# The second batch's sums of r*u*k made on TensorE per pair of heads, in a fused linear attention and gated feed-forward kernel

## The chip, the cores and the metric

The kernel runs on one core of one Trainium2 chip, as one launch. The metric is the device time of that launch in microseconds (us), the median of several runs. The engines are named as in the profile: PE is TensorE, DVE is VectorE, ACT is ScalarE, POOL is GpSimd, and SP issues the DMAs.

## The reference

Three layers follow each other on 4 batches of 768 tokens with 384 features. The change lies in the first, a linear attention with 8 heads of 48 features and a decaying state:

```python
for t in range(S):
    cur = einsum('bhd,bhe->bhde', u[None] * k_t, v_t)
    y[:, :, t] = einsum('bhd,bhde->bhe', r_t, state + cur)
    state = w_t[..., None] * state + einsum('bhd,bhe->bhde', k_t, v_t)
```

The token's own part, r_t times cur, is v_t times one number per token and head: the sum over the 48 features of r*u*k. These sums are what the change moves. Behind the attention come a feed-forward layer (h = gelu(x @ w_in), a layer norm of its second half, a 768x768 product over tokens, a gate, w_out, and a residual) and a second one (a sigmoid of a causal convolution with 5 taps, times x @ w_val, times w_out). All of it is fp32 to the reader; the large products are made as three products of split operands.

## The kernel before, in words

**Units and batches.** The attention is cut into units: one unit is one batch b, one segment s of 256 tokens (three per batch) and one pair p of heads (four), so 12 units per batch and 48 in all. Tokens of a segment lie in two tiles j of 128. Batch 0's attention runs first, with the loading and decoding of the weights and the start of its own feed-forward part beside it. After that `phase(b)` (L659) runs the feed-forward part of batch b, in the order of the words of `ORDER0`, `ORDER` or `LAST` (L646 to L657), and at each word `T` advances the attention of batch b + 1 by one tick. Batch 1's attention therefore runs beside batch 0's feed-forward part, which also still decodes weights (L144) and splits them into two parts (L161).

**The order of work.** The framework records the instructions, and a planner with a timing model orders each engine's queue by priorities and by when operands are ready in its model. `LEAD` (L112) moves the priority of each kind of step. On the chip each queue then runs in that order, and an instruction at its head that waits holds those behind it.

**One unit.** `unit` (L247) gives its steps. The packed tile `pk` holds decay, k and r with features on partitions. DVE makes the suffix products F (L271) and the prefix products E (L276), POOL makes r*E into L (L280), DVE (POOL for batch 0) makes k*F, called kh (L283). PE transposes kh (L297) and makes the scores (L303); ACT copies them, DVE masks (L311). In the next tick `kv` (L323) makes the chunk sums k*v on PE into one PSUM bank (L328), ACT copies them out (L347), a DVE scan runs the states (L353), ACT spreads them (L358), and another tick later PE makes the tokens' outputs (L372), which DVE adds to the tile `y` (L377). Batches 1 to 3 have two buffers for `pk`, and one for each of the two PSUM banks of `kv` and of the tokens.

**The token's own part** is made in two ways.
- Batch 0 (`first`): the step `q` makes r*k on DVE (L291), 128x256, in place over the decay part of `pk`. In `kv`, for each of the two tiles, PE multiplies it by a two-column matrix that holds u of the pair's two heads (L333), into columns of the same PSUM bank. The step `o` copies the four numbers per token out on ACT (L338), and POOL multiplies v by them into `y` (L342), 128x192 per unit.
- Batches 1 to 3: `bonus` (L222), once per tile of 128 tokens, six per batch, works on a tile `rk` with r and k of all heads, tokens on partitions. It is loaded by DMA (L220), into a single buffer. POOL makes r*k (L228), DVE multiplies by u (L229) and reduces over the features (L232), then the next load is issued, and POOL multiplies v by the sums into `y` (L236), 128x384 per tile. `begin` (L423) calls it for both tiles of a segment at its first pair.

**Queues and buffers nearby.** All DMAs are issued by SP, in its order: `pk`, `sv`, `v`, `rk`, weights and the output. `run_loads` (L396) issues the next load of a kind when its buffer's user is done. `y` and `v` have two buffers, one per segment. `y` is later transposed by PE for the feed-forward part (L470).

Of the kernel before, what the change touches and what calls it, by code (L numbers as in the profile page):

```python
# [26 lines left out]
SEG = 256  # L27
# [7 lines left out]
KS = S // 128  # L35
# [17 lines left out]
def tile_kernel(ctx, tc, pk, sv_, rk_, v_, u_, misc_, w_in, w_sgT, b_sg, w_o1, w_val,  # L53
# [39 lines left out]
    parts, at = {}, dict.fromkeys(ROOMS, 0)  # L93
# [9 lines left out]
    def buf(name, n, b=None):  # L103
        l = parts[name][min(units[n][0] if b is None else b, 1)]
        return l[n % len(l)]
# [20 lines left out]
    def leading(kind, f):  # L126
        def g(*args):
            with lead(kind):
                return f(*args)
        return g  # L130
# [44 lines left out]
    def load_weights(srcs, places):  # L175
        got = []
        for pl in dict.fromkeys(places):
            got += stage([s for s, p in zip(srcs, places) if p is pl], *pl)
        return got
# [33 lines left out]
    def load_nat(b, s):  # L213
        t = r2.tile([128, NT, DM], F32, tag="v", name="v")
        sp.dma_start(out=t, in_=v_[b, s * SEG:(s + 1) * SEG, :].rearrange("(j p) f -> p j f", p=128))
        vt[b, s] = t
# [5 lines left out]
    def bonus(b, i):  # L222

        s, j = divmod(i, NT)
        with lead("bon"):
            t = buf("rk", b * KS + i, b)
            q = t[:, 0:DM]
            pool.tensor_tensor(out=q, in0=q, in1=t[:, DM:2 * DM], op=ALU.mult)  # L228
            dve.tensor_tensor(out=q, in0=q, in1=u_bc, op=ALU.mult)  # L229
            hd = lambda a: a.rearrange("p (h d) -> p h d", d=D)  # L230
            rs = r2.tile([128, H], F32, tag="rsw", name="rs")
            dve.tensor_reduce(out=rs, in_=hd(q), op=ALU.add, axis=AX.X)  # L232
            run_loads("rk", b * KS + i + 1)
            if j == 0:
                yt[b, s] = ry.tile([128, NT, DM], F32, tag="y", name="y")
            pool.tensor_tensor(out=hd(yt[b, s][:, j, :]), in0=hd(vt[b, s][:, j, :]),  # L236
                               in1=rs.unsqueeze(2).to_broadcast([128, H, D]), op=ALU.mult)
# [9 lines left out]
    def unit(n):  # L247

        b, s, p = units[n]
        pkt = buf("pk", n)  # L250
        w, k, r = pkt[:, 0:OK_], pkt[:, OK_:OR_], pkt[:, OR_:OS_]
        kh, kn = buf("kh", n), buf("kn", n)
        sv = buf("sv", n).rearrange("p (c g e) -> p c g e", g=2, e=D)

        first = b == 0
        S = buf("SE", n).rearrange("p (c g e) -> p c g e", g=2, e=D)
        vcd = buf("vcd", n).rearrange("p (j c f) -> p j c f", j=NT, c=2)
        F, E, d1e = buf("F", n), buf("E", n), buf("D1E", n)  # L260
# [3 lines left out]
        half = [slice(0, 64), slice(64, 128)]  # L264
        e3 = E.rearrange("p (c t) -> p c t", t=W1)
        f3 = F[:, 1:NW + 1].rearrange("p (c t) -> p c t", t=W1)
        q = pkt[:, 0:SEG]
        t = {}

        def suffix():  # L270
# [48 lines left out]
        def warm(o, k):  # L319
            for _ in range(k if first else 0):  # L320
                pe.matmul(out=o[:, 256:512], lhsT=wsrc[:, 0:128], rhs=wsrc[:, 0:256], start=True, stop=True)

        def kv():  # L323
            t["b"] = ps(1, n, [128, 512])
            warm(t["b"], WB)
            for j in range(NT):
                for hh in range(2):
                    pe.matmul(out=t["b"][half[hh], 2 * j * D:(2 * j + 2) * D],  # L328
                              lhsT=kn[:, j * 128 + 64 * hh:j * 128 + 64 * hh + 64],
                              rhs=vcd[:, j, :, hh * D:(hh + 1) * D], start=True, stop=True)  # L330
            if first:
                for j in range(NT):
                    pe.matmul(out=t["b"][:, NC * D + 2 * j:NC * D + 2 * j + 2],  # L333
                              lhsT=q[:, j * 128:(j + 1) * 128], rhs=u_col[:, 2 * p:2 * p + 2], start=True, stop=True)
# [40 lines left out]
        def y_out():  # L375
# [3 lines left out]
        steps = {"F": suffix, "E": prefix, "L": r_part, "K": k_part, "D": chunk_decay, "q": ruk,  # L379
                "t": turn, "s": scores, "k": k_rows, "m": causal, "v": v_rows,  # L380
                "B": kv, "o": own_v, "d": kv_out, "a": states, "S": s_part, "p": keep,
                "C": tokens, "y": y_out}
        return {c: leading(c, f) for c, f in steps.items()}

    STAGES = "FELKD", "tskmv", "BdaSp", "Cy"

    def ps(i, n, shape):

        if units[n][0] == 0 and n % 2:
            return psC.tile(shape, F32, tag=f"c{i}", name=f"a{i}")  # L390
        return psA.tile(shape, F32, tag=f"a{i}", name=f"a{i}")

    loads = {"pk": load_unit, "sv": load_sv, "rk": load_rk}
    loaded, user = {"pk": 0, "sv": 0, "rk": KS}, {}

    def run_loads(kind, done, most=NU):  # L396

        while loaded[kind] < (B * KS if kind == "rk" else NU) and most > 0:
            n = loaded[kind]
            t = buf(kind, n, n // KS if kind == "rk" else None)  # L400
            if user.get(id(t), -1) >= done:
                break
            user[id(t)] = n
            loads[kind](n)
            loaded[kind] += 1
            most -= 1

    def attention(b):


        n0, n1 = b * NSEG * NP, (b + 1) * NSEG * NP
        if b == 0:
            first_loads()
        todo = {}

        def step(n, which):
            if n0 <= n < n1:
                if n not in todo:
                    todo[n] = unit(n)
                for c in which:  # L420
                    todo[n].pop(c)()

        def begin(n):  # L423
            if n < n1:
                _, s, p = units[n]
                step(n, STAGES[0])
                run_loads("pk", n + 1)
                if p == 0:
                    for j in range(NT):
                        bonus(b, s * NT + j)  # L430

        if b == 0:
            TICK = "F1 K1 E1 C-2 L1 q1 y-2 B-1 v1 d-1 o-1 t0 k0 s0 a-1 D1 S-1 p-1 m0"
            step(0, "FKEDLqv")
            for n in range(n0, n1 + 2):
                for w in TICK.split():
                    step(n + int(w[1:]), w[0])
                run_loads("sv", n - 1)
                run_loads("pk", min(n, n1))
                if 0 < n < n1 and units[n][2] == 0:  # L440
                    load_nat(*units[n + NP][0:2])
                yield
            return
        begin(n0)
        if n0 + NP < NU:
            load_nat(*units[n0 + NP][0:2])
        for n in range(n0, n1 + 2):
            for i in (2, 1, 0):
                step(n - i, STAGES[i + 1])
            run_loads("sv", n - 1)  # L450
            begin(n + 1)
            m = n + 1
            if m < min(n1, NU - NP) and units[m][2] == 0:
                load_nat(*units[m + NP][0:2])
            yield
# [203 lines left out]
    def phase(b):  # L659
        nx = b + 1 < B  # L660
        gen = attention(b + 1) if nx else None
        wgen = rest_of_weights() if b == 0 else iter(())
        own = {"u": u_step, "s": vs_step, "w": wo_step, "v": val_step, "o": out_step}
        for word in (ORDER0 if b == 0 else LAST if b == B - 1 else ORDER).split():
            kind, at = word[0], [int(x) for x in word[1:]]
            if kind in own:
                own[kind](b, *at)
                for _ in range(2):
                    next(wgen, None)
            elif kind == "i":  # L670
                x2_init(b, *at)
            elif kind == "c":
                for f in range(KD):
                    conv(b, at[0], f)
            elif nx:
                if kind == "T":
                    next(gen)
                elif kind == "n":
                    u_step(b + 1, 0, *at)
                else:  # L680
                    {"x": xT, "h": hv}[kind](b + 1, *at)
# [14 lines left out]
    def first_loads():  # L696
        ld = {"k": "pk", "s": "sv"}
        small = {"I": (ident, ident_), "M": (misc, misc_), "U": (u_bc, u_.to_broadcast([128, DM])),
                 "B": (b_bc, b_sg.to_broadcast([128, S]))}
        for c in "kMkvI s sk ks W kskvsk sks BU":  # L700
            if c in ld:
                run_loads(ld[c], 0, 1)
            elif c == "v":
                load_nat(0, len(vt))
            elif c in small:
                sp.dma_start(out=small[c][0], in_=small[c][1])
            elif c == "W":
                early["v"] = load_weights(cols(w_in, DV), [VN] * 3)
        for k in loads:
            run_loads(k, 0)  # L710

    att = attention(0)
    for n in range(14):
        next(att)
# [113 lines left out]
```

## Time and profile before

| what | value |
|---|---|
| runs of the kernel before (3) | median 584.35 us, 582.72 to 585.93 |
| the profiled execution, its own time | 586.35 us |
| its span, first to last instruction | 584.5 us |
| mean granted TensorE clock | 0.944 |
| PE busy | 524.6 us (90%), 4012 instructions |
| PE weight loads (PEld) busy | 446.8 us (76%), 4012 |
| DVE busy | 440.1 us (75%), 823 |
| ACT busy | 296.0 us (51%), 683 |
| POOL busy | 278.3 us (48%), 282 |
| moved by DMA | 55.76 MB, mean 95 GB/s |

The profile is of one execution, with every instruction's start and end on its engine. A busy PE is not PE at its peak, since matmuls are pipelined and their ends modelled. An instruction's time on DVE or POOL contains what it waits for inside it. Idle time ahead of an instruction is put down to whatever ended last before it. Line numbers are those of the kernel before; the names of tiles are given as output<-inputs.

### The profile page before, as it was taken

How to read it: one execution, taken by the hardware profiler on the slowest of the kernel's cores; microseconds unless marked ns; L12 is line 12 of the kernel's file. 1: busy time of each engine (PE TensorE's matmuls, PEld its weight loads, DVE VectorE, ACT ScalarE, POOL GpSimd, SP SyncE). 2: the span in 40 equal slices, each digit the busy share in tenths (PEclk: the TensorE clock that was granted, in tenths of full speed). 3: DMA queues.
4: the chain of work that ended last, by engine and by line, in shares of the span. 5: the costliest groups of instructions: out<-in, count | busy, mean ns of one | idle time of the engine just before them, and what ended most of it. 6: DMA issues, size and time to landing. Idle time of an engine off the chain costs nothing.

```text
span 584.5 us, 10613 instructions
## 1 busy us (share of the span) xinstructions
PE 524.6 (90%) x4012; PEld 446.8 (76%) x4012; DVE 440.1 (75%) x823; ACT 296.0 (51%) x683; POOL 278.3 (48%) x282
## 2 busy tenths in 40 slices
PE   8787888889747999889998998999999998999996
PEld 4565665788636898679877887889877887999985
DVE  7999999988997648993399659984399359523774
ACT  4766947542745435653365555654266635422233
POOL 7578845684666126662154126672154124722630
PEclk9899787978869999999997999899999999999999
DMA  8952444433434231342105351242104100000002
GB/s 313 385 218 56 150 151 121 151 109 108 123 91 139 85 107 42 96 127 77 42 9 156 96 156 34 60 159 82 42 15 116 61 16 0 28 14 1 1 0 81
DMA packets 27937, 55.76 MB, mean 95 GB/s; under 512 B 3184, under 2 KB 17264, under 8 KB 27888
## 3 DMA queue, kind: packets, MB, share of 16 engines
q1 hardware_dynamic: 27888, 55.11, 29.6%
q8 instruction: 31, 0.51, 0.4%
q14 instruction: 18, 0.15, 0.1%
HBM read 50.38 MB, written 4.72 MB: 94 GB/s over the span
## 4 chain that ended last, share of the span: by engine, by line
PE 48%; DVE 16%; issue 2%; ACT 1%; DMA 1%; POOL 1%; POOLq 0%; ACTq 0%
PE vps L514 13%; DVE cv L607 8%; PE ups L514 6%; PE c L578 6%; PE o L633 6%; PE val L514 4%; PE hv L491 4%; PE a L372 4%; PE a L303 2%; PE a L328 2%; DVE x L589 1%; PE a L297 1%; DVE SD L353 1%; DVE bs L497 1%; DVE vg L503 1%
## 5 line engine op out<-in xcount | busy, mean ns | idle before, releaser
L514 PE MATMUL vps<-wsg,vnt 128*128 128x384 f32 x576 | 116.7, 346 | 5.1 <-POOL wsg L164 3.2
L514 PEld LDWEIGHTS vps<-wsg,vnt 128*128 128x128 f32 x576 | 102.5, 193 | 8.3 <-POOL wsg L164 3.7
L565 POOL TENSOR_TENSOR gt<-gt,ut 128x384 f32<-128x384 f32 x32 | 35.0, 1096 | 110.5 <-DVE gt L554 90.2
L607 DVE SCALAR_TENSOR_TENSOR cv<-x,cw_col,cv 128x384 f32<-128x384 f32 x96 | 76.9, 835 | 0.0
L491 PE MATMUL hv<-win,x 128*128 128x512 f32 x216 | 64.9, 435 | 4.8 <-DVE cv L620 2.9
L578 PE MATMUL c<-gl,late 128*128 128x384 f32 x288 | 63.0, 348 | 1.6 <-DVE gl L568 1.3
L514 PE MATMUL ups<-x,win 128*128 128x384 f32 x288 | 61.4, 355 | 0.0
L358 ACT ACTIVATE SE<-SD 64x192 f32<-64x192 f32 x80 | 44.8, 560 | 28.1 <-DVE SD L353 13.2
L280 POOL TENSOR_TENSOR L<-pk,E 128x256 f32<-128x256 f32 x38 | 30.4, 800 | 51.1 <-PE a L372 32.9
L514 PEld LDWEIGHTS ups<-x,win 128*128 128x128 f32 x288 | 52.6, 196 | 1.8 <-DVE spare L151 0.2
L578 PEld LDWEIGHTS c<-gl,late 128*128 128x128 f32 x288 | 50.3, 191 | 3.9 <-DVE gl L568 1.4
L491 PEld LDWEIGHTS hv<-win,x 128*128 128x128 f32 x216 | 41.8, 204 | 14.1 <-DVE cv L620 3.3
L353 DVE TENSOR_TENSOR_SCAN SD<-SD,SD 128x288 f32<-128x288 f32 x48 | 46.1, 962 | 7.3 <-ACT SD L347 7.1
L514 PE MATMUL val<-x2hl,late 128*128 128x384 f32 x216 | 45.6, 354 | 3.0 <-DVE gt L554 2.8
L633 PE MATMUL o<-late,ml 128*128 128x384 f32 x216 | 44.0, 342 | 2.1 <-DVE ml L623 2.1
L316 ACT ACTIVATE vcd<-v 64x192 f32<-64x192 f32 x84 | 30.0, 357 | 28.8 <-PE a L328 28.2
L271 DVE TENSOR_TENSOR_SCAN F<-pk,D1F 128x260 f32<-128x260 f32 x40 | 36.4, 911 | 9.9 <-DMA pk<-in_pk_dram 6.9
L514 PEld LDWEIGHTS val<-x2hl,late 128*128 128x128 f32 x216 | 38.6, 195 | 6.2 <-issue 3.1
L372 PE MATMUL a<-SE,L 128*64 128x96 f32 x304 | 31.9, 276 | 12.1 <-DVE x L474 6.8
L567 ACT ACTIVATE gl<-gt 128x384 fp32r<-128x384 f32 x32 | 16.7, 523 | 50.7 <-POOL gt L565 47.0
L554 DVE SCALAR_TENSOR_TENSOR gt<-vps,misc,b_bc 128x384 f32<-128x384 f32 x32 | 19.5, 610 | 28.6 <-PE vps L514 27.0
L507 POOL TENSOR_TENSOR vnt<-vg,vnt 128x512 fp32r<-128x512 f32 x24 | 33.8, 1412 | 15.1 <-ACT vnt L506 15.0
(148 smaller groups left out, 1088.8 us busy)
## 6 DMA issues: line engine op xcount, KB each, us to landing
pk<-in_pk_dram SPq DMA_DIRECT2D x40, 386.5 KB, 3.4
sv<-in_sv_dram SPq DMA_DIRECT2D x39, 192.0 KB, 2.5
rk<-in_rk_dram SPq DMA_DIRECT2D x18, 384.0 KB, 3.2
v<-in_v_dram SPq DMA_DIRECT2D x12, 384.0 KB, 3.5
out_dram<-ot SPq DMA_DIRECT2D x24, 192.0 KB, 1.9
bits<-in_w_in_dram SPq DMA_DIRECT2D x6, 512.0 KB, 6.7
room_l<-in_pk_dram SPq DMA_DIRECT2D x7, 386.5 KB, 6.3
bits<-in_w_o_dram SPq DMA_DIRECT2D x7, 384.0 KB, 4.6
```

Source lines behind the costliest of these rows:

```text
L271: dve.tensor_tensor_scan(out=F[:, NW:0:-1], data0=w[:, NW:0:-1], data1=D1F[:, NW:0:-1], initial=0.0, op0=ALU.mult, op1=ALU.add)
L280: pool.tensor_tensor(out=ch(L[:, 0, :]), in0=ch(r), in1=e3[:, :, 0:C], op=ALU.mult)
L353: dve.tensor_tensor_scan(out=SD1, data0=SD1, data1=SD0, initial=0.0, op0=ALU.add, op1=ALU.mult)
L358: act.activation(out=S[half[hh], :, hh, :], func=AF.Copy, in_=d1[half[hh], :, 1:NC + 1].rearrange("p e c -> p c e"))
L372: pe.matmul(out=o, lhsT=L[:, i, c * C:(c + 1) * C], rhs=rhs[:, c], start=(i == 0), stop=(i == 1))
L491: pe.matmul(out=ps, lhsT=x[:, a, kk, j * 128:(j + 1) * 128], rhs=win[:, w, kk, DV:2 * DV], start=(z == 0), stop=(z == nmm - 1))
L507: pool.tensor_tensor(out=vnt[b][:, 1, i, :], in0=vg, in1=hi.bitcast(F32), op=ALU.subtract)]
L514: pe.matmul(out=ps, lhsT=lhs(a, kk), rhs=rhs(w, kk), start=(z == 0), stop=(z == nk * 3 - 1))
L565: pool.tensor_tensor(out=t, in0=t, in1=ut.pop((b, hf, d)), op=ALU.mult)
L578: pe.matmul(out=acc[0][f], lhsT=late["wo1"][:, a, d, f * 128:(f + 1) * 128], rhs=g[:, w, :], start=(d == 0 and q == 0), stop=(d == KV - 1 ...
L607: dve.scalar_tensor_tensor(out=t, in0=x2[:, f, k:k + HALF], scalar=cw_col[:, f, k:k + 1], in1=t, op0=ALU.mult, op1=ALU.add)
L633: pe.matmul(out=acc2[0][j], lhsT=m[:, a, j * 128:(j + 1) * 128], rhs=late["wo2"][:, w, g, :], start=(g == 0 and q == 0), stop=(g == KD - 1 ...
```

## The change

Batch 1 takes batch 0's way: its units get the steps `q` and `o`, and `bonus` runs for batches 2 and 3 only. The product r*k, which for batch 0 overwrites the decay in `pk`, goes for batch 1 into thirds of the single buffer of `rk`, unit n into third n modulo 3. The first load of `rk` is that of batch 2's first tile, and it is issued when batch 2's attention begins and no longer ahead of everything in `first_loads`. In batch 1 the step `q` comes right after the unit's other preparing steps, and `o` after the states of the same unit.

```diff
--- before.py
+++ after.py
@@ -254,7 +254,7 @@
-        first = b == 0
+        first, summed = b == 0, b < SUMMED
         S = buf("SE", n).rearrange("p (c g e) -> p c g e", g=2, e=D)
         vcd = buf("vcd", n).rearrange("p (j c f) -> p j c f", j=NT, c=2)
         F, E, d1e = buf("F", n), buf("E", n), buf("D1E", n)
@@ -264,7 +264,7 @@
         half = [slice(0, 64), slice(64, 128)]
         e3 = E.rearrange("p (c t) -> p c t", t=W1)
         f3 = F[:, 1:NW + 1].rearrange("p (c t) -> p c t", t=W1)
-        q = pkt[:, 0:SEG]
+        q = pkt[:, 0:SEG] if first else parts["rk"][1][0][:, n % 3 * SEG:(n % 3 + 1) * SEG]
         t = {}
         def suffix():
@@ -328,7 +328,7 @@
                     pe.matmul(out=t["b"][half[hh], 2 * j * D:(2 * j + 2) * D],
                               lhsT=kn[:, j * 128 + 64 * hh:j * 128 + 64 * hh + 64],
                               rhs=vcd[:, j, :, hh * D:(hh + 1) * D], start=True, stop=True)
-            if first:
+            if summed:
                 for j in range(NT):
                     pe.matmul(out=t["b"][:, NC * D + 2 * j:NC * D + 2 * j + 2],
                               lhsT=q[:, j * 128:(j + 1) * 128], rhs=u_col[:, 2 * p:2 * p + 2], start=True, stop=True)
@@ -382,6 +382,8 @@
                 "C": tokens, "y": y_out}
         return {c: leading(c, f) for c, f in steps.items()}
+
+    SUMMED = 2
     STAGES = "FELKD", "tskmv", "BdaSp", "Cy"
     def ps(i, n, shape):
@@ -391,7 +393,7 @@
         return psA.tile(shape, F32, tag=f"a{i}", name=f"a{i}")
     loads = {"pk": load_unit, "sv": load_sv, "rk": load_rk}
-    loaded, user = {"pk": 0, "sv": 0, "rk": KS}, {}
+    loaded, user = {"pk": 0, "sv": 0, "rk": SUMMED * KS}, {}
     def run_loads(kind, done, most=NU):
@@ -424,8 +426,10 @@
             if n < n1:
                 _, s, p = units[n]
                 step(n, STAGES[0])
+                if b < SUMMED:
+                    step(n, "q")
                 run_loads("pk", n + 1)
-                if p == 0:
+                if p == 0 and b >= SUMMED:
                     for j in range(NT):
                         bonus(b, s * NT + j)
@@ -441,12 +445,16 @@
                     load_nat(*units[n + NP][0:2])
                 yield
             return
+        if b == SUMMED:
+            run_loads("rk", 0)
         begin(n0)
         if n0 + NP < NU:
             load_nat(*units[n0 + NP][0:2])
         for n in range(n0, n1 + 2):
             for i in (2, 1, 0):
                 step(n - i, STAGES[i + 1])
+                if i == 1 and b < SUMMED:
+                    step(n - i, "o")
             run_loads("sv", n - 1)
             begin(n + 1)
             m = n + 1
@@ -706,7 +714,7 @@
                 sp.dma_start(out=small[c][0], in_=small[c][1])
             elif c == "W":
                 early["v"] = load_weights(cols(w_in, DV), [VN] * 3)
-        for k in loads:
+        for k in ("pk", "sv"):
             run_loads(k, 0)
     att = attention(0)
```

## Rows read from the trace of the kernel before

**Rows 1.** The page's part 2: busy tenths of PE and DVE in 40 slices of the span.
```profile
PE   8787888889747999889998998999999998999996
...
DVE  7999999988997648993399659984399359523774
```

**Rows 2.** Stretches (us): busy us and count of PE, PEld, DVE, ACT, POOL; PE clock, DMA.
```profile
41.00:75.00 34.00, 27.91 (x264) 20.77 (x266) 33.90 (x60) 25.99 (x65) 28.12 (x29) 0.85 0.29 89
75.00:195.00 120.00, 95.68 (x774) 78.37 (x772) 109.71 (x204) 63.88 (x147) 70.16 (x65) 0.86 0.41 126
195.00:225.00 30.00, 30.00 (x213) 26.27 (x212) 15.19 (x35) 12.10 (x27) 7.02 (x9) 1.00 0.25 80
225.00:253.00 28.00, 24.27 (x191) 18.75 (x190) 28.00 (x52) 17.76 (x40) 20.52 (x19) 1.00 0.27 79
```

**Rows 3.** Waits, 75 to 195 us: who waited for whom, us in total, times, longest.
```profile
PE a L372 <- DVE x L474: 6.8, 2, 3.9
...
PE a L297 <- DVE L L311: 4.1, 5, 1.9
...
PE vps L514 <- POOL wsg L164: 3.2, 2, 2.9
```

**Rows 4.** Stretches, DVE's instructions on the tile rk alone.
```profile
41.00:60.00 19.00, 0.72 (x1) 1.00 0.19 53
75.00:150.00 75.00, 7.70 (x11) 0.86 0.41 130
150.00:195.00 45.00, 4.32 (x5) 0.85 0.42 120
```

**Rows 5.** Waits again, 75 to 195 us: DVE's multiplication by u.
```profile
DVE rk L229 <- POOL rk L228: 3.4, 3, 2.2
```

**Rows 6.** Stretches, DVE: kh at L283 (first), and batch 0's r*k at L291.
```profile
75.00:195.00 120.00, 5.45 (x11) 0.86 0.41 126
...
0.00:75.00 75.00, 9.37 (x12) 0.89 0.63 219
```

**Rows 7.** Stretches, POOL: L228, L236, then batch 0's L342.
```profile
75.00:195.00 120.00, 9.42 (x8) 0.86 0.41 126
...
75.00:165.00 90.00, 6.28 (x6) 0.86 0.41 128
...
0.00:76.00 76.00, 9.45 (x12) 0.89 0.63 219
```

**Rows 8.** Timeline of POOL: start us, us, engine, line, operation, shapes, count.
```profile
161.93 2.32 POOL L236 TENSOR_TENSOR y<-v,rs 128x384 f32<-128x384 f32 x2
164.21 3.97 POOL L164 TENSOR_TENSOR wsg<-spare,wsg 128x384 fp32r<-128x384 f32 x3
```

**Rows 9.** Timeline of PE, at three places; idle time and its releaser in brackets.
```profile
60.20 0.61 PE L333 MATMUL a<-misc,pk 128*128 128x2 f32 x4
60.67 0.41 PE L297 MATMUL a<-ident,room_w 128*128 128x128 f32 x2
...
165.59 1.33 PE L514 MATMUL vps<-wsg,vnt 128*128 128x384 f32 x3 [2.86 <-POOL wsg L164]
...
211.13 0.55 PE L328 MATMUL a<-vcd,kn 128*64 128x96 f32 x8
```

**Rows 10.** Groups by form: busy us, mean ns of one, idle before.
```profile
L228 POOL TENSOR_TENSOR rk<-rk 128x384 f32<-128x384 f32 x18 | 19.9, 1104 | 21.8 <-DMA rk<-in_rk_dram 19.1 <-DVE E L276 2.7
...
L229 DVE TENSOR_TENSOR rk<-rk,u_bc 128x384 f32<-128x384 f32 x18 | 16.3, 908 | 7.6 <-POOL rk L228 7.6
...
L232 DVE TENSOR_REDUCE rs<-rk 128x8 f32<-128x384 f32 x18 | 9.6, 536 | 0.0
...
L338 ACT ACTIVATE rsw<-a 128x4 f32<-128x4 f32 x12 | 1.9, 170 | 0.0
```

**Rows 11.** Timeline of SP: its DMA issues.
```profile
139.17 0.33 SPq L220 DMA_DIRECT2D rk<-in_rk_dram  x1
140.59 1.28 SPq L139 DMA_DIRECT2D bits<-in_w_o_dram  x3
```

**Rows 12.** Timeline of DVE, at two places.
```profile
139.97 0.55 DVE L157 SCALAR_TENSOR_TENSOR spare<-bits,spare 128x384 int32<-128x384 int32 x1
...
264.56 0.56 DVE L229 TENSOR_TENSOR rk<-rk,u_bc 128x384 f32<-128x384 f32 x1 [2.90 <-POOL rk L228]
```

**Rows 13.** The page's part 6: KB of one transfer, median us to landing.
```profile
rk<-in_rk_dram SPq DMA_DIRECT2D x18, 384.0 KB, 3.2
```

**Rows 14.** The chain that ended last, 225 to 253 us: start us, us, what.
```profile
233.98 1.01 DVE rk L229
```

## The prediction, made before the changed kernel ran

> **What bounds the kernel now.** I read the page first: PE is busy in nearly every slice from a third of the way on, while in the slices from about 50 to 190 us it has gaps and it is DVE that is full [rows 1]. The table of stretches makes this exact [rows 2]. Between 75 and 195 us, where batch 0's feed-forward part runs beside batch 1's attention, DVE works 109.71 of 120 us and PE only 95.68; from 195 to 225 PE is full and DVE half idle; from 225 to 253 DVE is full again and PE is not. So the change, which touches batch 1 alone, falls where VectorE is the scarcest engine. What PE waits for there agrees: in the waits of that stretch PE's largest are on DVE's x (6.8 us), DVE's L (4.1) and POOL's wsg (3.2) [rows 3].
>
> **Removed from VectorE.** The old sums cost, per tile of 128 tokens, one multiplication by u (L229) and one reduction (L232). By the table of the tile rk, six pairs of batch 1 lie at 41 to 60 us (one multiplication, 0.72 us) and at 75 to 150 us (five multiplications and six reductions, 7.70 us together) [rows 4]. DVE also stood idle for 3.4 us, three times, until POOL's r*k had come [rows 5].
>
> **Added to VectorE.** Twelve products r*k of 128x256 (L291). The nearest row is DVE's kh multiplication, the same shape from SBUF in the same stretch: 5.45 us for 11, so 0.495 each. L291 itself in batch 0 cost 9.37 us for 12, 0.78 each [rows 6]. I take 0.495, the row of this stretch and this engine's load, so 5.9 us; the other end is 9.4, the 0.78.
>
> Batch 0's 0.78 is a mean of short and long ones. The Trainium skill, "SBUF — State Buffer", section "SBUF: two separate sides", says that a DVE instruction with two SBUF inputs and a GpSimd instruction that reads SBUF exclude each other for the whole of one of them. This speaks against the change: it issues twelve such DVE instructions for the six multiplications that it takes out, and as many POOL ones as before. By it the addition is nearer 9.4 us, and the net below shrinks by 3.5.
>
> **Moved.** The new r*k lies in the buffer of rk's tile, and batch 2's first load of rk is now issued at the start of batch 2's attention and must wait until batch 1's last sum has read that buffer. Before, three of batch 2's multiplications and two reductions were done ahead of 195 us: 4.32 us of DVE between 150 and 195 [rows 4]. They leave the stretch. Together DVE is relieved between 75 and 195 us of 7.7 + 3.4 + 4.3 - 5.9 = 9.5 us. What of it reaches the end lies between nothing and all of it. DVE is 91% full there, yet PE with its 95.68 us and the weights' loads limit the stretch too; I take half: **-4.7 us**. Of the pair at 41 to 60, where DVE was busy for 33.90 of the 34 us from 41 to 75 [rows 2], all counts: **-0.7**.
>
> **GpSimd.** Gone are batch 1's multiplications (9.42 us for eight in the stretch, 1.18 each, so 5.9 for five) and the six products with v, 6.28 us; added are twelve products with v of half the size, 9.45 us in batch 0 [rows 7]. The net is -2.7 us in a POOL that is busy for 70.16 of 120, so by itself nothing; but one place is on the path. At 161.93 two products with v run for 2.32 us right ahead of three weight splits [rows 8], and PE's next vps at 165.59 waited 2.86 us for such a split [rows 9]. The new products come unit by unit and one may stand there too, so I count half of 2.3: **-1.2**.
>
> **TensorE.** Four records per unit: in batch 0 they start at 60.20 and the next transpose at 60.67, so 0.47 us, 5.7 us for twelve units. Ten of the twelve fall before 195 us, where PE has 24 us of gaps that hide them; if that cover were gone they would cost 4.7. Units 22 and 23 (the latter's kv matmuls are at 211.13 [rows 9]) fall where PE is full: **+0.9**. The wait that PE gains, on r*k, has a tick of cover, since DVE makes it in the tick before; behind it on PE would queue the next transposes.
>
> **ScalarE, queues, buffers.** Twelve small copies of 0.17 us [rows 10] make 2.0 us on an ACT that is busy for 63.88 of 120 us: nothing; each stands ahead of the kv copy of its unit, so that chain grows by 0.47 + 0.17 us per unit, which twelve units spread over 120 us cover. On SP six loads go, each of which waited there for the last reduction; at 139.17 one held the queue, and the w_o loads at 140.59 came right behind [rows 11], but those need the decode of the weights before them, whose last L157 ended at 140.52 [rows 12], so nothing. v's buffer is now read one tick longer, so its reload, used four ticks later, comes about a tick later: nothing. The tile y is first written by POOL two ticks later than before, which only takes a wait away.
>
> **Batch 2's sums, given back.** The first load can go at about 211.7, when unit 23's matmuls are through. One tile then takes 3.2 us of load [rows 13], 1.1 of POOL, 0.9 and 0.54 of DVE [rows 10] and 0.3 of issue, 6.0 in all with one buffer. Two fit ahead of 225, where DVE is half idle; the third falls into the stretch where DVE is full and the chain of waits goes along it, through an L229 of 1.01 us for one [rows 14]: **+1.4**. The bounds are 0 and all three, 4.3.
>
> **Sum.** -0.7 - 4.7 - 1.2 + 0.9 + 1.4 = -4.3 us. The profiled execution took 586.35 us (span 584.5 and 1.85 around it), 2.0 above the median of the three runs, 584.35; I apply the difference to the median: **580.0 us**, 0.7% less. A measurement of this kernel can tell about 0.5% (2.9 us) from no change.
>
> **Rivals.**
> No change: VectorE's relief is not what ends last, because the weights' chain (load, decode, split, vps) and PE absorb it, and r*k costs its batch 0 price. For it: PE gaps on wsg, and DVE had 10 us of idle time in the stretch. Against it: x and L, both DVE's, are PE's longest waits. A quarter of 6.0 us is left, and half of the 1.2: -0.7 - 1.5 - 0.6 + 0.9 + 1.4 = -0.5, so 583.9 us. This is also where the exclusive ports of the skill's page lead.
>
> Slower: batch 2's sums come late. Its place is 212 to 253 us. With the buffer free only after batch 1's last unit, prefetching is lost, and DVE, which runs in order, waits for POOL's product inside its full stretch; such a wait of 2.90 us is there at 264.56 [rows 12]. It decides if fewer than two tiles are done by 225, that is, if the first load goes later than about 213. Price per tile in the stretch: 1.4 of DVE, 2.9 of waiting and 1.1 of POOL, which is itself busy for 20.52 of 28. Two tiles make 10.8; with the other terms (-5.7), +5.1: 589.4 us.
>
> A third, within both: the order of all engines is written anew by the planner from the changed costs, and a queue order that met its times by luck is lost; this can move the time by some us either way and widens the range.
>
> **Chances.** Forecast 0.47; no change 0.28; slower 0.25. The range: with all of DVE's relief and all of the 2.3 on the path the time is 584.35 - 0.7 - 9.5 - 2.3 + 0.9 = 572.8, and the slower rival gives 589.4; I take 572 to 590. By these cases faster by over 0.5% has 0.47, within 0.5% 0.28, slower 0.25.
>
> **What the next profile would show.** Twelve L229 and L232 instead of eighteen; twelve L291, L338 and L342 more; 48 more PE records at L333. Right would be: DVE below 101 us in its 120 us, the phase's end (the full stretch of PE) 4 to 6 us earlier, no L220 between 40 and 205 us. Step by step: L291 near 0.5 us between 75 and 195; the first load of rk for batch 2 near 207 to 212 and two reductions within 13 us of it. Wrong would be: r*k at 0.8 us or more, DVE idle on POOL's rk after 225, PE waiting at L333 for r*k, or a saving in batch 1's stretch that is gone by 265 us.

## Result and profile after

| kernel | runs | median us | ratio to before, 95% interval |
|---|---|---|---|
| after, first comparison | 4 | 577.40 (575.66 to 580.68) | 0.9884 [0.9844, 0.9924] |
| before, beside it | 4 | 585.14 (582.72 to 586.25) | |
| after, repeated later | 11 | 579.62 (575.81 to 582.51) | 0.9920 [0.9890, 0.9949] |
| before, beside the repeated one | 22 | 584.01 (581.76 to 589.72) | |

Forecast were 580.0 us and -0.7%; measured were -1.2% in the first comparison and -0.8% in the larger one. The median of all 15 runs of the changed kernel is 579.33 us. A ratio with its interval is the record's and goes by means, so it can differ a little from that of two medians. One run of the last experiment's six, at 582.84 us, was in a slower state and is left out of its median. Its profiled execution took 577.62 us (span 575.9, granted clock 0.946; before 586.35, 584.5, 0.944).

The page of the changed kernel, parts 1 and 2, against [rows 1]:

```profile
PE 526.2 (91%) x4060; PEld 451.1 (78%) x4060; DVE 436.1 (76%) x823; ACT 296.0 (51%) x695; POOL 275.9 (48%) x282
...
PE   8978788969989995998998998999989998999996
...
DVE  7999999899697679955399769985398449523674
```

There are 48 more PE records (4012 before), 12 more of ACT, and DVE has as many as before. The totals moved by 1.6 us on PE and 4.0 on DVE, so they do not explain 8 us; the stretches do. The table of stretches, columns as in [rows 2]:

```profile
41.00:75.00 34.00, 25.93 (x239) 19.23 (x238) 33.73 (x57) 24.47 (x59) 27.49 (x26) 0.80 0.30 100
75.00:195.00 120.00, 110.70 (x901) 92.97 (x900) 103.00 (x205) 67.88 (x169) 64.25 (x63) 0.92 0.33 101
195.00:225.00 30.00, 25.84 (x209) 21.69 (x207) 23.91 (x48) 15.68 (x36) 15.96 (x17) 0.98 0.28 89
225.00:253.00 28.00, 26.04 (x180) 21.83 (x181) 25.13 (x51) 15.94 (x37) 19.26 (x19) 0.90 0.29 92
```

Between 75 and 195 us PE now issues 901 matmuls where it issued 774, and DVE is busy 6.7 us less. From 41 to 75 nothing is relieved: DVE is as full as before (33.73 for 33.90) and PE does less. Then PE is no longer full from 195 to 225: a part of what was won is given back there. The granted clock from 75 to 195 is 0.92 for 0.86 before; what share of the gain is the clock's and what share is waits that went was not separated.

DVE's instructions on the tile rk by stretch, against [rows 4] (columns: length, busy us and count, PE clock, DMA):

```profile
41.00:60.00 19.00, 0.00 (x0) 0.86 0.13 39
75.00:150.00 75.00, 3.53 (x6) 0.87 0.34 105
150.00:195.00 45.00, 1.64 (x4) 1.00 0.32 94
195.00:225.00 30.00, 2.46 (x3) 0.98 0.28 89
225.00:253.00 28.00, 3.17 (x6) 0.90 0.29 92
```

Between 75 and 195 us these are the new r*k alone: 5.17 us for ten (the other two run just ahead of 75). The instructions that they stand for took 0.72 + 7.70 us, and batch 2's early ones, which have moved, 4.32. By form, all executions of the new parts (columns: shortest, median and longest in ns, first and last start):

```profile
L291 DVE TENSOR_TENSOR rk<-pk x12: 391/462/836, 70.2 to 186.3; 128x256 f32<-128x256 f32 x12
...
L333 PE MATMUL a<-misc,rk x48: 168/251/375, 91.7 to 205.9; 128*128 128x2 f32 x48
```

The waits from 75 to 195 us, against [rows 3] (who waited for whom; us in total, times, longest):

```profile
POOL y L342 <- ACT rsw L338: 19.1, 9, 5.6
...
PE a L372 <- DVE y L377: 5.3, 1, 5.3
...
ACT SD L347 <- PE a L333: 2.8, 1, 2.8
...
PE a L297 <- DVE L L311: 1.4, 1, 1.4
```

PE's wait for DVE's x at L372 (6.8 us) and that of its vps matmuls for the wsg splits (3.2) are gone, the one for L is a third of what it was, the one for y has grown (5.3, before 1.7 in one wait), and there is none at L333 for r*k. New too is that POOL stands for 19.1 us ahead of its products with v until ACT has copied the sums out of PSUM.

The timeline of the changed kernel: POOL's last wsg splits, against [rows 8], then batch 2's first sums (SP's loads, DVE):

```profile
146.46 2.00 POOL L164 TENSOR_TENSOR wsg<-spare,wsg 128x384 fp32r<-128x384 f32 x2
149.47 1.03 POOL L164 TENSOR_TENSOR wsg<-spare,wsg 128x384 fp32r<-128x384 f32 x1
150.75 2.30 POOL L164 TENSOR_TENSOR wsg<-spare,wsg 128x384 fp32r<-128x384 f32 x2 [0.26 <-ACT wsg L163]
153.37 1.02 POOL L164 TENSOR_TENSOR wsg<-spare,wsg 128x384 fp32r<-128x384 f32 x1 [0.31 <-ACT wsg L163]
...
206.45 0.38 SPq L220 DMA_DIRECT2D rk<-in_rk_dram  x1
213.59 0.33 SPq L220 DMA_DIRECT2D rk<-in_rk_dram  x1
227.40 11.04 SPq L220 DMA_DIRECT2D rk<-in_rk_dram  x2
...
212.01 0.56 DVE L229 TENSOR_TENSOR rk<-rk,u_bc 128x384 f32<-128x384 f32 x1 [0.51 <-POOL rk L228]
212.98 0.54 DVE L232 TENSOR_REDUCE rs<-rk 128x8 f32<-128x384 f32 x1
...
226.80 0.54 DVE L232 TENSOR_REDUCE rs<-rk 128x8 f32<-128x384 f32 x1
```

The six splits that lay between 154.9 and 178.5 us are through in one go by 154.4. Batch 2 has one tile's sums done by 225 us, not two.

How far each kernel is at five marks shows where time is won and lost (starts in us, each from one execution; "wsg" is POOL's eighth wsg split; "gate" DVE's multiplication for the gate, L554 of before; "last y" DVE's L377 of batch 1's last unit):

| kernel | last w_in split | wsg | 5th gate | last y of batch 1 | 9th gate | span |
|---|---|---|---|---|---|---|
| before | 82.4 | 164.2 | 181.8 | 218.5 | 265.0 | 584.5 |
| after | 72.8 | 147.4 | 161.0 | 214.1 | 260.4 | 575.9 |
| after, repeated | 72.6 | 145.0 | 158.5 | 212.2 | 258.4 | 573.8 |

After is 20.8 us ahead at the fifth gate and 4.4 to 4.6 us at the next two marks; the rest of the 8.6 us in span comes after 260 us. The part from the ninth gate to the end took 319.4 us before, and 315.4 and 315.5 after. The two executions of the same kernel differ by 2 to 2.5 us at every mark but the first, so no mark is better than that.

### The profile page after: what moved, and what is told of

Read it like the earlier page. It is cut to its first block, busy times and chain, and to the rows that moved or that the text cites. A ratio compares the mean times of both kernels' runs of the same rounds, so it can differ in the third digit from the quotient of the medians.

```text
span 575.9 us, 10711 instructions
## 1 busy us (share of the span) xinstructions
PE 526.2 (91%) x4060; PEld 451.1 (78%) x4060; DVE 436.1 (76%) x823; ACT 296.0 (51%) x695; POOL 275.9 (48%) x282
## 4 chain that ended last, share of the span: by engine, by line
PE 47%; DVE 34%; DMA 9%; issue 4%; ACT 3%; POOL 2%; SPq 1%; POOLq 0%; DVEq 0%; ACTq 0%
PE vps L522 12%; DVE cv L615 10%; PE c L586 6%; PE ups L522 5%; PE a L372 5%; PE o L641 5%; PE hv L499 4%; PE val L522 3%; DVE SD L353 3%; DVE F L271 2%; PE a L303 2%; PE a L328 2%; DMA pk<-in_pk_dram 2%; DMA rk<-in_rk_dram 2%; DVE x L597 1%
## 5 line engine op out<-in xcount | busy, mean ns | idle before, releaser
L522 PE MATMUL vps<-wsg,vnt 128*128 128x384 f32 x576 | 112.3, 339 | 0.0
L522 PEld LDWEIGHTS vps<-wsg,vnt 128*128 128x128 f32 x576 | 100.1, 188 | 1.5
L499 PE MATMUL hv<-win,x 128*128 128x512 f32 x216 | 66.9, 438 | 5.4 <-DVE cv L628 2.7
L353 DVE TENSOR_TENSOR_SCAN SD<-SD,SD 128x288 f32<-128x288 f32 x48 | 43.7, 911 | 6.5 <-ACT SD L347 6.3
L522 PE MATMUL val<-x2hl,late 128*128 128x384 f32 x216 | 44.2, 346 | 3.7 <-DVE gt L562 2.5
L372 PE MATMUL a<-SE,L 128*64 128x96 f32 x304 | 33.2, 277 | 8.9 <-DVE y L377 7.4
L576 DVE TENSOR_TENSOR gl<-gt,gl 128x384 fp32r<-128x384 f32 x32 | 19.5, 611 | 28.7 <-ACT gl L575 28.7
L271 DVE TENSOR_TENSOR_SCAN F<-pk,D1F 128x260 f32<-128x260 f32 x40 | 32.4, 810 | 10.4 <-DMA pk<-in_pk_dram 7.4
```

What stands on the lines that cost most here:

```text
L271: dve.tensor_tensor_scan(out=F[:, NW:0:-1], data0=w[:, NW:0:-1], data1=D1F[:, NW:0:-1], initial=0.0, op0=ALU.mult, op1=ALU.add)
L353: dve.tensor_tensor_scan(out=SD1, data0=SD1, data1=SD0, initial=0.0, op0=ALU.add, op1=ALU.mult)
L372: pe.matmul(out=o, lhsT=L[:, i, c * C:(c + 1) * C], rhs=rhs[:, c], start=(i == 0), stop=(i == 1))
L499: pe.matmul(out=ps, lhsT=x[:, a, kk, j * 128:(j + 1) * 128], rhs=win[:, w, kk, DV:2 * DV], start=(z == 0), stop=(z == nmm - 1))
L522: pe.matmul(out=ps, lhsT=lhs(a, kk), rhs=rhs(w, kk), start=(z == 0), stop=(z == nk * 3 - 1))
```

## Experiments

**1 and 2. How much is in the loads.** With `SUMMED = 1` the changed code sums batch 1 the old way, but its first rk load is written at batch 1's attention, and not ahead of everything (the first kernel). In the second, batch 2's first load is also written at batch 2's attention.

```diff
-    SUMMED = 2
+    SUMMED = 1
```
```diff
-            run_loads("rk", b * KS + i + 1)
+            if (b, i) != (1, KS - 1):
+                run_loads("rk", b * KS + i + 1)
...
-        if b == SUMMED:
-            run_loads("rk", 0)
+        if b in (SUMMED, 2):
+            run_loads("rk", b * KS)
```

> The changed kernel with SUMMED = 1: batch 1 keeps its old sums on GpSimd and VectorE; all that is left of the change is that the first load of rk is issued when batch 1's attention begins and not among the first loads. Theory A (the gain is VectorE's and GpSimd's relief from batch 1's sums): within 0.5% of before, 583 to 587 us, and batch 0's later vs steps (the 5th to the 8th gt) not earlier by more than 3 us. Theory B (the early load and its product held back the decode of the weights, and the planner's new order alone pays): 578 to 581 us, with the wsg splits done by about 155 us as in the changed kernel.

> As s1_load_late, and batch 2's first load of rk is also issued only when batch 2's attention begins. The difference between the two is the moved part of the prediction alone: its step counted -2.2 us (half of 4.3) in batch 0's phase and +1.4 later, so -0.7 us net: the two within 2 us of each other. If prefetching those sums matters (the slower rival), this one is 3 to 5 us longer than s1_load_late.

Measured: 581.20 us (12 runs), 0.9943 [0.9918, 0.9968], and 579.34 (8 runs), 0.9922 [0.9893, 0.9950]; before beside both 584.23 (25 runs). The second edit did not do what it was written for. Batch 2's first load is the seventh of rk, and SP issued it at the same place in both kernels (the first, then the second):

```profile
148.36 0.33 SPq L220 DMA_DIRECT2D rk<-in_rk_dram  x1
...
148.43 0.33 SPq L220 DMA_DIRECT2D rk<-in_rk_dram  x1
```

The planner had moved it forward again, right behind batch 1's last reduction (147.9 to 148.4 us in the second). The two profiles show the same instructions in the same order on TensorE, ScalarE, GpSimd and SP, and on VectorE but for one pair that changes places between the two executions of after, too; so the two kernels count as one here, with 20 runs and a median of 580.83 us, 3.4 us under before. Their medians of 12 and 8 runs lie 1.9 us apart: with so few runs, a difference of that size is not told from chance. More than half of the gain is there with not one sum moved to TensorE, and what batch 2's late load costs was not tested by them. At the ninth gate (263.7 and 262.7 us) these kernels are only 1 to 2.5 us ahead of before, of 5.0 and 7.8 us in span; the rest comes behind it. POOL's timeline of the first one, its w_in splits and its first product:

```profile
56.55 1.44 POOL L164 TENSOR_TENSOR win<-spare,win 128x512 fp32r<-128x512 f32 x1 [1.26 <-ACT win L163]
60.29 1.19 POOL L228 TENSOR_TENSOR rk<-rk 128x384 f32<-128x384 f32 x1
...
74.91 1.67 POOL L164 TENSOR_TENSOR win<-spare,win 128x512 fp32r<-128x512 f32 x1
```

and the same of the kernel before:

```profile
40.97 1.17 POOL L228 TENSOR_TENSOR rk<-rk 128x384 f32<-128x384 f32 x1
...
65.02 1.46 POOL L164 TENSOR_TENSOR win<-spare,win 128x512 fp32r<-128x512 f32 x1
...
82.39 1.67 POOL L164 TENSOR_TENSOR win<-spare,win 128x512 fp32r<-128x512 f32 x1
```

Before, the load went at 22.53 us, ahead of w_in's second three at 28.62; here it goes at 31.15, behind them. The w_in splits come 8.5 and 7.5 us earlier.

**3. The sums gone.** The changed kernel without batch 1's r*k, its sums and their products with v; y is a copy. Batch 2's first three rk loads go early here, at 30.38, 82.77 and 95.66 us, since nothing else uses the buffer.

```diff
-            if summed:
+            if first:
...
-                if b < SUMMED:
-                    step(n, "q")
...
-                if i == 1 and b < SUMMED:
-                    step(n - i, "o")
```

> The changed kernel without batch 1's sums: no r*k, no TensorE sums, no copy and no product with v for batch 1, whose outputs lack the token's own part (y is written by a copy). What the removal alone gives. Theory A: the new parts cost 6.6 us of VectorE and 11.6 of GpSimd in the full stretch, so leaving them out gains 3 to 5 us more: 572 to 575 us. Theory B: the old sums were no bound, nor are the new ones: 576 to 579, like the changed kernel.

Measured: 574.92 us (6 runs), 0.9849 [0.9811, 0.9887]. Against the kernel above, which has batch 1's load late, the old sums, and batch 2's first three loads ahead of 195 us as well, removing the old sums is worth 5.9 us. Against the 15 runs of after, the new sums, with batch 2's sums behind 200 us, cost 4.4 us (2.5 against the first four).

**4. The third batch too.** `SUMMED = 3`.

> SUMMED = 3: batch 2's sums come from TensorE too, in the phase where TensorE is nearly full. By the prediction's way of reckoning: 5.7 us more of TensorE where it is the bound, against two tiles' VectorE work in the full stretch after 225 us and the waits there, about 4 to 6 us; so within 0.5% of the changed kernel, 575 to 580 us. Theory B says the same or slower, by up to 5 us.

Measured: 581.89 us (12 runs), 0.9956 [0.9928, 0.9984], so 2.3 us over the repeated after, with intervals that overlap. Its stretch from 225 to 253 us:

```profile
225.00:253.00 28.00, 28.00 (x195) 24.31 (x194) 18.60 (x43) 15.25 (x35) 12.88 (x14) 0.94 0.13 43
```

DVE loses a quarter of its work there (25.13 to 18.60) and PE becomes full. From batch 1's last y to the ninth gate the kernel takes 39.2 us for after's 46.4. But from batch 2's last y to the 17th gate it takes 47.0 for 38.7, and the lead is gone. There batch 3's sums start late: its first rk load goes at 333.48 us, in after at 261.81. So the time is no better, a miss for the expectation, not because nothing was won in this stretch but because as much was lost in the next one like it; what part of that is the late load's was not separated.

**5 and 6. Load or product.** To the changed kernel an rk load that nobody needs is given back its old place among the first loads; and in the kernel before, the load stays and only POOL's first product of batch 1 is placed behind a later instruction.

```diff
             run_loads(k, 0)
+        t = parts["rk"][1][0].rearrange("p (two f) -> p two f", two=2)
+        sp.dma_start(out=t, in_=rk_[1, 0:128, :, :])
```
```diff
-            pool.tensor_tensor(out=q, in0=q, in1=t[:, DM:2 * DM], op=ALU.mult)
+            with ExitStack() as behind:
+                if (b, i) == (1, 0):
+                    behind.enter_context(tc.issue_after(last[2][2].ins))
+                pool.tensor_tensor(out=q, in0=q, in1=t[:, DM:2 * DM], op=ALU.mult)
```

> The changed kernel with one load of a tile of rk put back where before has it, among the first loads; nothing computes on it, and batch 1's first r*k overwrites it. Theory B1 (the 0.4 MB among the first loads is what s1_load_late gains from: it sets back the w_in loads behind it and with them the decode of the second half of w_in): 579.5 to 581.5 us, some 3 us of the changed kernel's 7 lost, with the last win split back at 80 to 83 us. Theory B2 (not the load, but its product on GpSimd and VectorE at 41 to 44 us): like the changed kernel, 576.5 to 578.5.

> The kernel before, where only the first product r*k of batch 1 on GpSimd is put behind the split of hv's third tile (so from 41 us to about 75 to 90 us); its load stays among the first loads. Theory B1: like before, 583 to 586 us. Theory B2: like s1_load_late, 580 to 582 us.

Measured: 581.95 us (12 runs), 0.9954 [0.9928, 0.9980], and 581.78 (12 runs), 0.9951 [0.9917, 0.9985]; before 584.11 (29 runs). Timeline of the first, SP and POOL:

```profile
22.16 0.33 SPq L720 DMA_DIRECT2D rk<-in_rk_dram  x1
...
28.26 1.82 SPq L139 DMA_DIRECT2D bits<-in_w_in_dram  x3
...
63.84 1.72 POOL L164 TENSOR_TENSOR win<-spare,win 128x512 fp32r<-128x512 f32 x1
...
82.12 1.27 POOL L164 TENSOR_TENSOR win<-spare,win 128x512 fp32r<-128x512 f32 x1 [1.29 <-ACT win L163]
```

One load of 384 KB puts the w_in splits back to where they were, and takes some 2 us of the gain (2.3 by the medians against the repeated after, 2.0 by the ratios, whose intervals overlap). That the load delays w_in is shown; by what chain this reaches the end is not, since this kernel's wsg splits were among the earliest (from 138.7). The second kernel's POOL timeline:

```profile
81.42 1.26 POOL L164 TENSOR_TENSOR win<-spare,win 128x512 fp32r<-128x512 f32 x1
...
84.97 1.44 POOL L231 TENSOR_TENSOR rk<-rk 128x384 f32<-128x384 f32 x1
...
151.78 1.34 POOL L164 TENSOR_TENSOR wsg<-spare,wsg 128x384 fp32r<-128x384 f32 x1
```

Nothing is removed here and w_in stays late, but the product goes from 40.97 to 84.97 and the eighth wsg split comes at 151.78 for 164.2; 2.3 us are won. This is the new order by itself.

**7 and 10. r*k on GpSimd.** The changed kernel, with batch 1's r*k moved to POOL.

```diff
-            dve.tensor_tensor(out=q, in0=r, in1=k, op=ALU.mult)
+            (dve if first else pool).tensor_tensor(out=q, in0=r, in1=k, op=ALU.mult)
```

> The changed kernel with batch 1's r*k on GpSimd and not on VectorE: VectorE loses 6.6 us (twelve of 0.55), GpSimd gains about 9.6 (twelve of 0.8, as r*E costs there). Theory A (VectorE is the scarcest engine of batch 0's phase): 575 to 577 us, 0.5 to 2 us less than the changed kernel. Rival (GpSimd's order decides: it waited 19 us for the small copies in that stretch, and collides with VectorE): 577 to 580.

> The changed kernel with batch 1's r*k on GpSimd, once more, beside the changed kernel itself. Theory A: 1 to 3 us less than after_again. If only the order of the queues differs by chance: within 1 us of it or more.

Measured: 576.54 us (6 runs), 0.9842 [0.9795, 0.9889], and on the chip of the repeated after 575.55 (6 runs), 0.9861 [0.9824, 0.9898], 4.1 us under that one. It beats before in both comparisons, and the changed kernel in the second; in the first the intervals of the two overlap. Its r*k by form (the second time):

```profile
L291 POOL TENSOR_TENSOR rk<-pk x12: 736/1054/1190, 69.3 to 184.4; 128x256 f32<-128x256 f32 x12
```

its waits from 75 to 195 us:

```profile
POOL y L342 <- ACT rsw L338: 6.0, 4, 2.6
```

and that stretch:

```profile
75.00:195.00 120.00, 110.18 (x910) 91.61 (x908) 106.58 (x197) 67.91 (x169) 74.58 (x75) 0.94 0.32 102
```

POOL takes twice as long for it as DVE, but from time in which it stood waiting: 19.1 us of waits for rsw become 6.0.

**8. r*k twice on VectorE.**

```diff
-            dve.tensor_tensor(out=q, in0=r, in1=k, op=ALU.mult)
+            for _ in range(1 if first else 2):
+                dve.tensor_tensor(out=q, in0=r, in1=k, op=ALU.mult)
```

> The changed kernel with each of batch 1's r*k made twice on VectorE, 6.6 us more in batch 0's phase. Theory A with the prediction's share of a half: 3.3 us more than the changed kernel, 580 to 581.5 us. If VectorE's relief does not reach the end: within 1 us of it, 576.5 to 578.5.

Measured: 581.36 us (12 runs), 0.9968 [0.9935, 1.0002], 1.7 us over the repeated after and 4.0 over its first four runs, with an interval that overlaps that of the former. DVE's r*k of batch 1 in this kernel, then in after:

```profile
60.00:200.00 140.00, 14.80 (x24) 0.84 0.33 107
...
60.00:200.00 140.00, 6.64 (x12) 0.90 0.34 106
```

The added DVE work is 8.2 us, more than a second 6.6, and 1.7 to 4.0 us of it reach the end: a share of 0.2 to 0.5.

**9 and 11. After again, and TensorE's sums twice.**

```diff
-                for j in range(NT):
+                for j in [*range(NT)] * (1 if first else 2):
```

> The changed kernel itself, unedited, beside q_on_pool on one chip, for a firmer time of it: 576.5 to 578.5 us, 1.0 to 1.3% less than before. If its place near 577 was partly the chance of four runs, 579 to 580.

> The changed kernel with each of batch 1's sums made twice on TensorE: 48 more records, 5.7 us of TensorE at 0.47 us per unit. The prediction's step (only the units in the stretch where TensorE is full pay, 0.9 us): 577.5 to 579.5. If all of it is on the path: 583.

Measured: 579.62 us, as above, and 580.53 (12 runs), 0.9940 [0.9915, 0.9965]: 0.9 us for 48 more records, which is not told from nothing, but is well below the 5.7 us that they last.

**12. One old multiplication gone.** The kernel before without L229 for batch 1, so that its sums lack u.

```diff
-            dve.tensor_tensor(out=q, in0=q, in1=u_bc, op=ALU.mult)
+            if b != 1:
+                dve.tensor_tensor(out=q, in0=q, in1=u_bc, op=ALU.mult)
```

> The kernel before without the multiplication by u for batch 1 (so its own part is wrong by that factor): six instructions of 0.9 us less on VectorE, 5.3 us with the first at 43 us, and nothing else taken away. Theory A with a share of a half to 0.6, as q_twice had (4.0 us for 6.6): 2.6 to 3.2 us less than before, 580.5 to 582.5. If VectorE's load is not what counts in the kernel before but the order of loads and weights: within 1.5 us of before, 583 to 585.5.

Measured: 576.18 us (5 runs), 0.9857 [0.9814, 0.9901], 7.8 us under before (584.01, 22 runs) where 2.6 to 3.2 were expected. The stretch from 75 to 195 us:

```profile
75.00:195.00 120.00, 103.23 (x841) 87.70 (x840) 108.20 (x202) 66.02 (x153) 72.97 (x66) 0.90 0.40 128
```

Some 5 us of DVE's work, in six multiplications, bring more than their own length, and in the same stretch: PE issues 841 matmuls for 774. The rest comes, it may be argued, with the order that the planner writes for the other costs, or with the granted clock (0.90 for 0.86); which part is which was not separated.

## Why the prediction was right, and where not

Direction and size were right: -0.7% was forecast for -0.8% (-1.2% in the first four runs). VectorE's full stretch from 75 to 195 us is where time is won, but the lead of 20.8 us at the fifth gate is down to 4.4 at batch 1's last y, and about half of the gain in span shows only behind 260 us. The composition was wrong, and the closeness of the sum is in good part luck. The prediction's terms, sorted by the kernels that carry them:

| step | predicted us | measured us |
|---|---|---|
| first load and product later, old sums kept: the pair at 41 to 60 (-0.7), the load nothing | -0.7 | -3.4 (584.23 to 580.83, 20 runs) |
| old sums removed: half of 7.7 + 3.4, and GpSimd's -1.2 | -6.7 | -5.9 (580.83 to the kernel without sums, 574.92) |
| new sums in, batch 2's sums moved: half of 5.9, TensorE's +0.9, half of 4.3 taken off, +1.4 given back | +3.1 | +4.4 (+2.5 in the first comparison) |
| all | -4.3 | -4.9 (584.23 to 579.33) |

Each measured step is a difference of two medians, by the intervals uncertain by about 1.5 us (the first) to 2.8, and the third goes across comparisons. The second and third rows together are the exchange of the sums that the change is named for: -3.6 was forecast, by the rival of no change it would be +0.2, and -1.5 is left (580.83 to 579.33), less than the 1.9 us between the first two kernels. By these medians the first row brought 2.7 us more than forecast and the exchange 2.1 less, and the two errors happened to cancel. The first row depends on the order of the steps too: the early load is worth 0.57 and 0.78% when it goes first (with its product), and 0.34% when it goes last (0.9954 to 0.9920).

**The step that failed** is the pair at 41 to 60, -0.7. It counted one DVE multiplication and looked for SP's loads in the later stretch alone ("six loads go"). The load itself stood at 22.53 us ahead of w_in's second three, and its way to the end was costed at nothing; moving load and product behind them brought 3.4 us, though the multiplication was not gone there but only moved, from 43.4 to 64.7 us in the first kernel. The prediction's "nothing" for queues looked only behind 75 us.

**VectorE's relief.** Half of its time was taken to reach the end. Doubling r*k gave a share of 0.2 to 0.5, and moving it away gains 4.1 us for 6.6: half lies within what these show. The one removal by itself, without u, gained more than all of it. DVE was to be below 101 us of 120 and is at 103.00: without those on the tile rk it has 195 instructions in the stretch where it had 188, so more of the other work now fits in. Busy time in a fixed stretch was a poor mark, the 901 matmuls in it are the better one.

**r*k.** Taken at 0.495 us for the stretch, the ten in it took 0.517 each; all twelve took 0.554 on average, 0.391 at the least and 0.836 at the most. The Trainium skill, "SBUF — State Buffer", section "SBUF: two separate sides", says that such a DVE instruction and one of GpSimd that reads SBUF exclude each other. The trace agrees in part: the four that ran with no GpSimd instruction beside them took 391 to 427 ns, and the six that took 498 ns or more all had one beside them, but two that had one took 400 and 414. The 0.78 us of batch 0 did not come.

**GpSimd.** The wsg splits are no longer waited for, as predicted, but not because two products ahead of them went: they come 8 to 25 us earlier, and in the kernel with the moved product, too. The term's size cannot be told apart from the order.

**TensorE.** +0.9 was forecast, and its doubling cost 0.9, which is not told from nothing. Two units' sums fell behind 195 us, as forecast, at 198.1 and 205.5; none waited for r*k.

**Batch 2's sums.** The first load went at 206.45, forecast for 207 to 212. The second reduction came at 226.80, 20 us behind that load where 13 were forecast, so the point from which the slower rival was to decide was passed, and the forecast sign of it came too. The waits from 225 to 265 us:

```profile
DVE rk L229 <- POOL rk L228: 5.1, 2, 3.5
```

Yet the rival's 10.8 us are not there. From batch 1's last y to the ninth gate after took 46.4 us and 46.1 repeated, before 46.5 and the kernel without sums 45.4, and the last two have batch 2's first three loads ahead of 195 us: by these single executions the late sums cost about 1 us at most at that place. The rival took DVE to be full from 225 to 253 as it was before, and now DVE is busy there for 25.13 of 28. No run holds back this load alone, so its price by itself stays open; the third batch's kernel shows that the same lateness may cost more elsewhere.

**The planner's order**, the third rival, is part of the result and not only of its uncertainty: 2.3 us by the medians for one product moved, and more than the work removed in the kernel without u. The phase's end came 4.4 us earlier, as forecast (4 to 6), and 6.3 in the repeated execution. What lies behind 260 us, another 4 us, is in both executions of after and in the first two kernels (315.8 and 314.0 us from the ninth gate to the end), but from the 48th y to the 25th gate alone they took 32.4 and 33.9 us (before 34.0), so a part of it belongs to the execution.

**What stays open**: through which chain the early load reaches the end; how much of the gains of the first, sixth and twelfth kernels is the order that the planner happens to write, and how much the granted clock; what batch 2's late sums cost by themselves; and whether the exchange of the sums, the load's place apart, gains anything.

## What to carry to other kernels

When a step is moved out of a batch, find its first load and first product in the start-up, however short they are, and see what stands behind them: here that was worth more than the exchange of the sums. Work put back took three quarters of what the removal had won (4.4 of 5.9 us); ask first whether an idle engine can take it, even at twice the duration. Look in the trace whether an edit moved what it was to move, since a planner can put it back where it was. A forecast of the net can be right with wrong terms, so build the steps one at a time before the terms are carried over.

## What the runs showed that was not expected

- One load of 384 KB issued at 22.16 us moved weight splits by 7.6 us at 56.21 and 9.3 us at 72.8 (after against the kernel with that load), though its issue took 0.33 us.
- The same r*k of 128x256 took 391 to 836 ns on DVE and 736 to 1190 ns on POOL.
- Matmuls with two columns of output against 128x128 weights in fp32 lasted 168 to 375 ns each, beside a weight load of 186 to 333; a unit's four took 0.47 us and in one place 0.87.
- The granted clock is not a property of the kernel alone: two executions of after had 0.946 and 0.958 on average, with spans of 575.9 and 573.8 us. The stretch from 286 to 339 us, for one, had 0.97 and 1.00.
